# Attention probabilities turned in one step, one batch's queries loaded in 128-byte blocks, and a new count of warm matmuls in the opening

## The chip, the cores and the metric

The kernel runs on one core of a Trainium2 chip. TensorE (PE) multiplies matrices into PSUM, VectorE (DVE) and ScalarE (ACT) do what is done element by element, GpSimd (POOL) a few subtractions, and SyncE (SP) issues the DMAs. The metric is the device time of one execution in microseconds (us), as the median of several runs.

## The reference

Two attentions in a row, then a mixture of experts with one expert per token. B=8, H=8, S=576, D=64, 32 packs; the experts take 512 features through F=1024, E=8.

```
p_packed = softmax(scale * p @ k.T) @ v          # 32 packs attend to 576 keys
x        = softmax(scale * q @ p_packed.T) @ p_packed
for each token s of batch b:
    fresh  = argmax(x[b, s] @ w_gate)
    e      = fresh if s == 0 or sigmoid(x[b, s] @ w_local) < 0.5 else expert of token s-1
    prob   = softmax(x[b, s] @ w_gate)[e]
    out[b, s] = prob * (relu(x[b, s] @ w1[e]) @ w2[e])
```

## The kernel before

All eight batches go through one pipeline. For each batch, whose tokens take one expert in the usual case, the kernel does not form x. It packs the expert's W1 with the attended packs (`pack_weights`: ppT times a 512-wide half of W1, a "pack", L783; ACT rounds it to wph at L790, DVE keeps the rest as wpl at L793), so that layer 1 multiplies the query probabilities a2 straight into the packed weights. Both sides are kept as a high and a low part (a2h, a2l; wph, wpl), so one half of a 128-wide chunk of layer 1 is six matmuls (L806, "a six"). Its relu gives h (high part on ACT L816, low part on DVE L821). W2 is split likewise (ACT L832, DVE L834), and layer 2 sums h times W2 into five accumulators acc0 to acc4 (L845, L850, L854). A batch has eight chunks, each with two sixes and five blocks of layer 2.

Beside these main matmuls PE does the next batches' attention, as side work:

- `scores` (L415): packs times keys, into two banks.
- `keys`: exp of the scores (ACT L448), then the probabilities are turned, 2 times 3 transposes of 128 by 96 (L458), each three into one PSUM bank, copied by ACT (L460) to a1T; times the values (L470, "av"); divided on DVE into zz (L478); turned on PE (L485) and copied to ppT.
- `queries`: query scores (L511, L520), DVE transposes to sT (L529), maximum (L540), subtraction (L542), exp on ACT (L544), sum (L548, L550, L552), division (L554), transposes into a2t (L560), then a2h (ACT L568) and a2l (L571; on DVE for batch 0, on POOL for the others).
- Queries and keys come to PE with their features on the partitions. For batches 0 and 1 they are loaded as tokens, rows of 1536 bytes (`load_tokens`, L274), and turned by PE three transposes at a time (`turn_tokens`, L365) with an ACT copy (L369); for later batches they are loaded as blocks in runs of 128 bytes (`load_blocks`, four DMAs at L288) and turned by DVE (`turn_keys`, `turn_queries`).

PSUM has three working banks, bank0 to bank2, and the five accumulators; before batch 0's main matmuls begin, the accumulators serve as further banks. A bank is free again when what reads it is done. The order on each engine is fixed when the kernel is built: `weave` runs all of these as generators, each of which says with `need` what it waits for (tiles, buffers, so many banks), and a planner (`Clock`) that prices each instruction gives the time at which each could go on. The main thread `chunks` is taken when it is ready, the side threads when their time has come and a credit allows. Anything that alters one planned time can alter the order from there on. Before batch 0's main matmuls begin, `weave` also fills PE's planned pauses with `keep_warm(n)`: n matmuls of a zero tile (L214), whose results are not used.

`FIRST_W2` holds back loads: in batch 0 the pieces of W2 from number 2 on wait for batch 1's values, those from number 4 on for its queries; in batch 1 the values and queries wait for as many pieces of W2.

Of the kernel before, what the change touches and what calls it, by code (L numbers as in the profile page):

```python
# [38 lines left out]
WARM, FILL = 10, 400.0  # L39
# [119 lines left out]
def packed_attn_moe_kernel(  # L159
# [156 lines left out]
    def loads(st):  # L316
# [11 lines left out]
        else:  # L328
            if isinstance(b, int):
                yield need(when=lambda: "loaded" in sts[b - 1] and (b < 2 or "ereg" in sts[b - 2]))  # L330
            order = (("p", 1), ("k", 0), ("k", 1), ("v", 0), ("v", 1), ("q", 0), ("q", 1)) if st["second"] else \
                (("v", 0), ("v", 1), ("p", 1), ("k", 1), ("q", 1))
        for name, Q in order:
            blocks = name in "kq" and not (st["early"] or st["second"])
            if st["second"] and name in FIRST_W2:
                yield need(when=lambda: len(sts[0].get("w2", ())) >= FIRST_W2[name])
            yield need(slot="p_in" if name == "p" else "qn" if blocks else "kv")
            if name == "p":
                st["p"] = load_packs_by_half(b)
                continue  # L340
            x = {"k": k, "v": v, "q": q}[name]
            if blocks:
                st[name] = load_blocks(x, b)
            else:
                st[name, Q] = load_tokens(x, b, Q)
# [96 lines left out]
    def keys(st, Q):  # L442
# [11 lines left out]
        for r in range(2):  # L454
            yield need(sc, banks=1, when=lambda: not st["early"] or st["weighed"] == NQ)
            tp = bank()
            for j in range(J3):
                nc.tensor.transpose(out=tp[:TP, 128 * j:128 * j + 128], in_=chunks[:, (J3 * r + j) // 2, (J3 * r + j) % 2], identity=ident)  # L458
            copy = nc.vector.tensor_copy if st["early"] and r == 1 else nc.scalar.copy
            copy(out=a1T[:, J3 * r:J3 * r + J3], in_=tp[:TP, :128 * J3].rearrange("a (j x) -> a j x", j=J3))  # L460
            give(tp)
        give(sc)
# [36 lines left out]
    def queries(st, Q):  # L499
# [56 lines left out]
        for r in range(2):  # L556
            if st["early"] or st["second"]:
# [190 lines left out]
    def weights(st):  # L748
# [10 lines left out]
        for c in range(NC):  # L759
            if st.get("early"):  # L760

                yield need(when=lambda: all(c < n or (x, 1) in sts[1] for x, n in FIRST_W2.items()))
# [186 lines left out]
    def weave(main):  # L949
# [3 lines left out]
        while main in threads or any(x.batch < 0 for x in threads):  # L953
# [4 lines left out]
            while started < B and started <= max(at_batch[0], 0) + AHEAD:  # L958
# [3 lines left out]
                    *((turn_keys(st, 0), turn_keys(st, 1)) if started != 1 else (turn_keys(st, 0), turn_tokens(st, "k"))), scores(st, 0), scores(st, 1), keys(st, 0), keys(st, 1), gate_weights(st) if started == 0 else None, gates(st), *((turn_queries(st, 0), turn_queries(st, 1)) if started > 1 else (turn_tokens(st, "q"),)), queries(st, 0), queries(st, 1),  # L962
# [17 lines left out]
            if x is None:  # L980
                x = min(when, key=when.get)
                if at_batch[0] < 0:
                    keep_warm(max(0, int((when[x] - now) / FILL)))
# [113 lines left out]
```

## Time and profile before

| | before |
|---|---|
| median of 3 runs | 440.71 us (440.34 to 441.14) |
| the profiled execution | 440.03 us, its span 438.2 us |
| PE busy | 417.8 us, 95% |
| DVE busy | 303.9 us, 69% |
| ACT busy | 183.5 us, 42% |
| mean granted clock of PE | 0.984 |
| chain that ended last | PE 88%, DVE 5%, DMA 3% |

The span is cut at PE's work by the profile: a row of the views below gives an instruction (or a run of alike ones), its start in us from the span's start, its duration, its line in the code, and in brackets how long the engine stood idle just before it and what ended that. Busy times of PE in a row overlap with those of its neighbours, since matmuls are pipelined; what a group takes is read from start to start. The granted clock is 1.00 at 2.4 GHz and 0.50 at 1.2 GHz. A matmul in float32 has several records: a warm matmul has two.

### The profile page before, as it was taken

The page shows a single profiled execution, that of the slowest core. Times are in us where ns is not written, and L with a number is a line of the kernel's source. Part 1 is how long each engine was busy: PE and PEld are TensorE (multiplying, and loading weights), DVE is VectorE, ACT ScalarE, POOL GpSimd, SP SyncE. Part 2 cuts the span into 40 slices and gives each one's busy share as a digit, 9 for nine tenths or more (in the row PEclk, how much of TensorE's full clock was granted, in tenths as well). Part 3 has the DMA queues.
Part 4 walks back from the last instruction along what each step waited for, and adds up shares of the span by engine and source line. Part 5 has one row for each costly group of instructions (what it writes and reads, how often), then busy time and mean ns, then how long its engine had stood idle before and what let it go on. Part 6 is the DMA issues. An engine that isn't in the chain of part 4 may idle for free.

```text
span 438.2 us, 10127 instructions
## 1 busy us (share of the span) xinstructions
PE 417.8 (95%) x3928; PEld 326.9 (75%) x3929; DVE 303.9 (69%) x831; ACT 183.5 (42%) x424; POOL 24.9 (6%) x41
## 2 busy tenths in 40 slices
PE   7968999999999999999999999999999999999993
PEld 6756778758866787588876787587876788688882
DVE  4587469876986798648984898648985798444331
ACT  1544534454435553535425553435424453443231
POOL 0000002100110011000110011000110002000000
PEclk9896999999999999999999999999999999999998
DMA  8989699899939995999269991999455210921003
GB/s 191 233 266 259 174 148 137 327 182 226 96 121 321 133 142 179 349 131 194 94 220 240 177 194 49 347 140 141 157 187 186 81 43 10 351 96 37 0 1 114
DMA packets 153942, 73.16 MB, mean 167 GB/s; under 512 B 123680, under 2 KB 132896, under 8 KB 153888
## 3 DMA queue, kind: packets, MB, share of 16 engines
q1 hardware_dynamic: 151760, 72.30, 75.5%
q8 instruction: 33, 0.54, 0.6%
q10 hardware_dynamic: 2128, 0.15, 0.4%
q14 instruction: 21, 0.17, 0.2%
HBM read 63.00 MB, written 9.44 MB: 165 GB/s over the span
## 4 chain that ended last, share of the span: by engine, by line
PE 88%; DVE 5%; DMA 3%; issue 1%; ACT 1%; SPq 0%; POOLq 0%; DVEq 0%; POOL 0%; ACTq 0%
PE acc L845 40%; PE bank L806 24%; PE acc L850 4%; PE bank L783 3%; DMA kv<-in_k_dram 3%; PE acc L854 3%; PE bank L470 3%; PE bank L415 2%; PE bank L458 2%; PE bank L511 2%; PE bank L658 1%; DVE wpl L793 1%; PE bank L365 1%; DVE a2t L560 1%; PE acc L214 0%
## 5 line engine op out<-in xcount | busy, mean ns | idle before, releaser
L845 PE MATMUL acc<-w2s,h 128*128 128x512 f32 x768 | 207.7, 402 | 0.0
L845 PEld LDWEIGHTS acc<-w2s,h 128*128 128x128 f32 x768 | 135.1, 188 | 30.6 <-issue 8.3
L816 ACT ACTIVATE h<-bank 128x288 fp32r<-128x288 f32 x128 | 52.7, 412 | 117.9 <-PE bank L806 108.1
L821 DVE SCALAR_TENSOR_TENSOR h<-bank,h 128x288 fp32r<-128x288 f32 (+2 forms) x192 | 61.3, 347 | 50.1 <-ACT h L816 49.3
L806 PEld LDWEIGHTS bank<-a2h,wph 128*128 128x128 f32 x256 | 47.0, 191 | 23.9 <-issue 3.6
L806 PE MATMUL bank<-a2h,wph 128*128 128x288 f32 x256 | 57.9, 308 | 5.5 <-DVE wpl L793 1.8
L806 PE MATMUL bank<-a2l,wph 128*128 128x288 f32 x256 | 55.5, 299 | 0.0
L806 PE MATMUL bank<-a2h,wpl 128*128 128x288 f32 x256 | 55.3, 298 | 0.0
L834 DVE TENSOR_TENSOR w2s<-w2raw,w2s 128x512 fp32r<-128x512 f32 x64 | 47.7, 745 | 8.3 <-ACT w2s L832 8.2
L806 PEld LDWEIGHTS bank<-a2l,wph 128*128 128x128 f32 x256 | 41.7, 191 | 0.0
L806 PEld LDWEIGHTS bank<-a2h,wpl 128*128 128x128 f32 x256 | 41.7, 191 | 0.0
L832 ACT CAST w2s<-w2raw 128x512 fp32r<-128x512 f32 x64 | 39.4, 616 | 0.2
L571 POOL TENSOR_TENSOR a2l<-a2t,a2h 128x576 fp32r<-128x576 f32 x14 | 20.5, 1462 | 328.7 <-ACT a2h L568 328.7
L793 DVE TENSOR_TENSOR wpl<-bank,wph 128x512 fp32r<-128x512 f32 x31 | 20.1, 685 | 13.3 <-ACT wph L790 13.3
L790 ACT CAST wph<-bank 128x512 fp32r<-128x512 f32 x31 | 16.7, 590 | 28.0 <-PE bank L783 26.9
L850 PE MATMUL acc<-w2s,h 128*128 128x512 f32 x64 | 26.9, 420 | 0.0
L854 PE MATMUL acc<-w2s,h 128*64 128x512 f32 x64 | 25.3, 395 | 0.0
L783 PE MATMUL bank<-w1t,ppT 64*32 64x512 f32 x248 | 17.4, 601 | 2.7 <-DVE sm L550 1.6
L529 DVE STREAM_TRANSPOSE sT<-bank 128x288 f32<-128x288 f32 x30 | 12.8, 462 | 10.1 <-ACT gate L527 9.4
L448 ACT ACTIVATE a<-a,nb 128x576 f32<-128x576 f32 x16 | 12.5, 779 | 14.9 <-DVE nb L433 14.9
L460 ACT COPY a1T<-bank 96x384 f32<-96x384 f32 x28 | 13.3, 477 | 10.5 <-PE bank L458 10.0
L383 DVE STREAM_TRANSPOSE qn<-qn 128x1152 f32<-128x1152 f32 x12 | 16.4, 1364 | 0.1
(146 smaller groups left out, 434.7 us busy)
## 6 DMA issues: line engine op xcount, KB each, us to landing
w1t<-in_moe_w_dram SPq DMA_DIRECT2D x16, 1024.0 KB, 6.3
w2raw<-in_moe_w_dram SPq DMA_DIRECT2D x64, 256.0 KB, 7.7
kv<-in_v_dram SPq DMA_DIRECT2D x16, 576.0 KB, 10.7
out_dram<-o SPq DMA_DIRECT2D x32, 256.0 KB, 3.8
qn<-in_k_dram SPq DMA_DIRECT2D x24, 288.0 KB, 7.5
qn<-in_q_dram SPq DMA_DIRECT2D x24, 288.0 KB, 6.9
kv<-in_k_dram SPq DMA_DIRECT2D x4, 576.0 KB, 6.9
kv<-in_q_dram SPq DMA_DIRECT2D x4, 576.0 KB, 11.2
```

Source lines behind the costliest of these rows:

```text
L571: eng.tensor_tensor(out=a2l, in0=a2t, in1=a2h.bitcast(F32), op=ALU.subtract)
L783: nc.tensor.matmul(out=ts[Q][32 * h:32 * h + 32, :], lhsT=st["ppT"][Q][rows, 32 * h:32 * h + 32], rhs=w1t[rows, h], start=True, stop=True,)
L790: nc.scalar.copy(out=hi[:, Q], in_=ts[Q])
L793: nc.vector.tensor_tensor(out=lo[:, Q], in0=ts[Q], in1=hi[:, Q].bitcast(F32), op=ALU.subtract)
L806: nc.tensor.matmul(out=t[:, :HALF], lhsT=st["wp"][c // 4][wi][:, Q, fs], rhs=a2[ai][Q][:, ts], start=(n == 0), stop=(n == 5),)
L816: nc.scalar.activation(out=h[:, HALF * half:HALF * half + HALF], in_=t[:, :HALF], func=AF.Relu)
L821: nc.vector.scalar_tensor_tensor(out=h[:, dst:dst + z - a], in0=t[:, a:z], scalar=0.0, in1=h[:, HALF * half + a:HALF * half + z].bitcast(F32),
L832: nc.scalar.copy(out=w[:, 0], in_=raw)
L834: nc.vector.tensor_tensor(out=w[:, 1], in0=raw, in1=w[:, 0].bitcast(F32), op=ALU.subtract)
L845: nc.tensor.matmul(out=acc, lhsT=hs[hi], rhs=w[:, wi], start=(c == 0 and n == 0), stop=(c == NC - 1 and n == 2),)
L850: nc.tensor.matmul(out=acc, lhsT=h[:, 512:S + TAIL], rhs=w[:, 0], start=(c == 0), stop=False, skip_group_check=True,)
L854: nc.tensor.matmul(out=acc[0:TAIL], lhsT=h[:, 512:S], rhs=w[:, 1], start=False, stop=(c == NC - 1), skip_group_check=True,)
```

## The change

1. `keys` turns both halves of the probabilities in one step: it asks for two banks at once, issues the six transposes in a row into both, and then the two copies. Before, each half asked for one bank, was turned and copied, and only then the other.
2. Batch 1's queries are loaded as blocks and turned by DVE (`turn_queries`), as in later batches, in place of tokens turned by PE. Two "kv" buffers are no longer used for them, one "qn" buffer is. The layout of a2t for batch 1 follows. The condition that holds back W2's pieces of batch 0 names the new load. Batch 1's keys stay tokens.
3. Before batch 0's main matmuls, the number of warm matmuls is the time from PE's planned end (no longer from `now`) to the next planned step, divided by 240 in place of 400.

```diff
-WARM, FILL = 10, 400.0
+WARM, FILL = 10, 240.0
...
-            order = (("p", 1), ("k", 0), ("k", 1), ("v", 0), ("v", 1), ("q", 0), ("q", 1)) if st["second"] else \
+            order = (("p", 1), ("k", 0), ("k", 1), ("v", 0), ("v", 1), ("q", 1)) if st["second"] else \
                 (("v", 0), ("v", 1), ("p", 1), ("k", 1), ("q", 1))
         for name, Q in order:
-            blocks = name in "kq" and not (st["early"] or st["second"])
+            blocks = name in "kq" and not st["early"] and not (st["second"] and name == "k")
...
-        for r in range(2):
-            yield need(sc, banks=1, when=lambda: not st["early"] or st["weighed"] == NQ)
+        def turned(r):
             tp = bank()
             for j in range(J3):
                 nc.tensor.transpose(out=tp[:TP, 128 * j:128 * j + 128], in_=chunks[:, (J3 * r + j) // 2, (J3 * r + j) % 2], identity=ident)
+            return tp
+
+        def copied(r, tp):
             copy = nc.vector.tensor_copy if st["early"] and r == 1 else nc.scalar.copy
             copy(out=a1T[:, J3 * r:J3 * r + J3], in_=tp[:TP, :128 * J3].rearrange("a (j x) -> a j x", j=J3))
             give(tp)
+
+
+        yield need(sc, banks=2, when=lambda: not st["early"] or st["weighed"] == NQ)
+        for r, tp in enumerate([turned(r) for r in range(2)]):
+            copied(r, tp)
         give(sc)
...
-            if st["early"] or st["second"]:
+            if st["early"]:
...
-                yield need(when=lambda: all(c < n or (x, 1) in sts[1] for x, n in FIRST_W2.items()))
+                yield need(when=lambda: all(c < n or x in sts[1] for x, n in ((("v", 1), FIRST_W2["v"]), ("q", FIRST_W2["q"]))))
...
-                    ... ((turn_queries(st, 0), turn_queries(st, 1)) if started > 1 else (turn_tokens(st, "q"),)), ...
+                    ... ((turn_queries(st, 0), turn_queries(st, 1)) if started else (turn_tokens(st, "q"),)), ...
...
-                    keep_warm(max(0, int((when[x] - now) / FILL)))
+                    keep_warm(max(0, int((when[x] - clock.engine("PE")) / FILL)))
```

In the new kernel the lines behind `keys` are numbered seven higher (L783 becomes L790, L806 L813, L845 L852, and so on; the turn L458 is L457). The planner puts the work in another order nearly everywhere. Three places follow, by the fixed order of the two kernels; a row is a line, an operation, what it writes, what it reads, its shape, and how many stand in a row.

On PE, batch 0's two packs and the first six of layer 1, before (L783 the pack, the two halves of W1 being w1t_451 and w1t_453; L214 warm matmuls):

```order
L365 MATMUL bank2_513<-ident_77,kv_315 128x96 x3
L214 MATMUL acc4_66<-warm_64 128x128
L783 MATMUL bank0_535<-w1t_451,ppT_313 32x512 x4
L783 MATMUL acc1_536<-w1t_451,ppT_324 32x512 x4
L214 MATMUL acc4_66<-warm_64 128x128 x5
L783 MATMUL bank1_565<-w1t_453,ppT_313 32x512 x4
L783 MATMUL bank2_566<-w1t_453,ppT_324 32x512 x4
L806 MATMUL bank0_583<-a2h_123,wph_533 128x288
```

and now:

```order
L365 MATMUL acc1_561<-ident_77,kv_333 128x96 x3
L790 MATMUL bank0_567<-w1t_470,ppT_331 32x512 x4
L790 MATMUL bank1_568<-w1t_470,ppT_342 32x512 x4
L214 MATMUL acc4_66<-warm_64 128x128 x10
L790 MATMUL bank2_620<-w1t_472,ppT_331 32x512 x4
L790 MATMUL bank0_621<-w1t_472,ppT_342 32x512 x4
L813 MATMUL bank1_632<-a2h_123,wph_565 128x288
```

Ten warm matmuls stand between the packs where five did, and the last quarter goes to bank0, which the first quarter of the first pack wrote; before, no bank came twice.

On DVE, what follows batch 0's a2t at the same place, before (wpl the packs' low parts, w2s the low part of W2's first piece, h the first relu):

```order
L560 STREAM_TRANSPOSE a2t_122<-sT_406 128x3x96 x2
L571 TENSOR_TENSOR a2l_125<-a2t_121,a2h_123 128x576
L571 TENSOR_TENSOR a2l_126<-a2t_122,a2h_124 128x576
L793 TENSOR_TENSOR wpl_534<-bank0_535,wph_533 128x512
L793 TENSOR_TENSOR wpl_534<-acc1_536,wph_533 128x512
L793 TENSOR_TENSOR wpl_564<-bank1_565,wph_563 128x512
L793 TENSOR_TENSOR wpl_564<-bank2_566,wph_563 128x512
L834 TENSOR_TENSOR w2s_590<-w2raw_455,w2s_590 128x512
L821 SCALAR_TENSOR_TENSOR h_562<-bank0_583,h_562 128x288
```

and now:

```order
L567 STREAM_TRANSPOSE a2t_122<-sT_436 128x3x96 x2
L578 TENSOR_TENSOR a2l_125<-a2t_121,a2h_123 128x576
L578 TENSOR_TENSOR a2l_126<-a2t_122,a2h_124 128x576
L800 TENSOR_TENSOR wpl_566<-bank0_567,wph_565 128x512
L800 TENSOR_TENSOR wpl_566<-bank1_568,wph_565 128x512
L841 TENSOR_TENSOR w2s_639<-w2raw_474,w2s_639 128x512
L800 TENSOR_TENSOR wpl_615<-bank2_620,wph_614 128x512
L800 TENSOR_TENSOR wpl_615<-bank0_621,wph_614 128x512
L828 SCALAR_TENSOR_TENSOR h_613<-bank1_632,h_613 128x288
```

W2's low part moved from behind the last two wpl to ahead of them. Further up on DVE, the maximum of the first quarter's scores moved ahead of the transposes of the second quarter's.

On PE, batch 1's attention beside batch 0's second chunk of layer 2 (L458 a turn, L365 queries' tokens, L470 av, L485 the turn of zz), before:

```order
L458 MATMUL bank2_778<-ident_77,a1_579 96x128 x3
L365 MATMUL bank1_788<-ident_77,kv_478 128x96 x3
L845 MATMUL acc0_643<-w2s_630,h_601 128x512 x3
L470 MATMUL bank2_795<-kv_461,a1T_758 32x64 x24
L365 MATMUL bank1_824<-ident_77,kv_478 128x96 x3
L845 MATMUL acc1_662<-w2s_630,h_601 128x512 x3
L485 MATMUL bank2_848<-ident_77,zz_820 128x128
L365 MATMUL bank0_853<-ident_77,kv_518 128x96 x3
L845 MATMUL acc2_680<-w2s_630,h_601 128x512 x3
```

and now:

```order
L492 MATMUL bank2_812<-ident_77,zz_800 128x128
L852 MATMUL acc0_693<-w2s_681,h_653 128x512 x3
L457 MATMUL bank1_821<-ident_77,a1_618 96x128 x3
L457 MATMUL bank2_825<-ident_77,a1_618 96x128 x3
L852 MATMUL acc1_712<-w2s_681,h_653 128x512 x3
L852 MATMUL acc2_730<-w2s_681,h_653 128x512 x3
L477 MATMUL bank0_843<-kv_480,a1T_816 32x64 x24
```

The token transposes are gone, the two threes of the turn stand together, and two blocks of layer 2 lie between them and the av that reads their copies. In all, the order of before has 11 of 18 turns with their halves side by side, that of now all 18; warm matmuls ahead of the first scores go from 19 to 30. At the seam between batches 0 and 1 the new order has both packs of batch 1 in batch 0's last half chunk, the first on bank0 and bank1, the second on bank2 and bank0; in batches 3 to 6 the order is now the same from batch to batch. On SP, the values of batch 2 follow W2's pieces directly.

## Rows read from the trace of the kernel before

**Rows 1.** The page, part 1: engine, busy us, share of the span, instructions.
```profile
PE 417.8 (95%) x3928; PEld 326.9 (75%) x3929; DVE 303.9 (69%) x831; ACT 183.5 (42%) x424; POOL 24.9 (6%) x41
```

**Rows 2.** By stretch: length, each engine's busy us, PEclk, DMA share, GB/s.
```profile
11.50:14.80 3.30, 3.30 (x27) 2.87 (x14) 1.29 (x8) 2.21 (x5) 0.00 (x0) 0.50 1.10 235
28.60:35.30 6.70, 3.50 (x42) 1.62 (x42) 6.55 (x14) 4.59 (x11) 0.00 (x0) 1.00 1.06 350
35.40:42.10 6.70, 5.95 (x50) 5.57 (x51) 4.80 (x11) 2.17 (x5) 0.00 (x0) 0.50 1.08 262
50.00:60.00 10.00, 8.76 (x122) 7.10 (x121) 3.74 (x10) 4.57 (x14) 0.00 (x0) 1.00 0.79 151
135.00:430.00 295.00, 293.80 (x2545) 230.86 (x2544) 206.53 (x540) 127.17 (x288) 16.14 (x20) 1.00 0.69 152
```

**Rows 3.** PE's waits: line, releaser, us in total, times, longest us.
```profile
PE bank L806 <- DVE zz L478: 1.4, 3, 0.5
...
PE bank L806 <- DVE df L716: 0.8, 1, 0.8
PE bank L806 <- ACT qn L369: 0.7, 1, 0.7
...
PE bank L806 <- ACT a1T L460: 0.5, 1, 0.5
```

**Rows 4.** PE in time, opening: start, us, engine, line, tiles, count [idle <- releaser].
```profile
1.09 6.18 PE L214 MATMUL acc<-warm 128*128 128x128 f32 x38 [1.09 <-DVE warm L207]
8.80 1.15 PE L415 MATMUL acc<-kv,p_in 32*32 32x192 f32 x48 [1.53 <-DVE p_in L351]
...
23.57 0.44 PE L365 MATMUL acc<-ident,kv 96*128 96x96 f32 x3 [1.28 <-DMA kv<-in_k_dram]
```

**Rows 5.** PE in time, first packs and first layers.
```profile
33.54 1.09 PE L783 MATMUL bank<-w1t,ppT 64*32 64x512 f32 x16 [1.10 <-DMA w1t<-in_moe_w_dram]
36.15 0.82 PE L806 MATMUL bank<-a2h,wph 128*128 128x288 f32 x2 [1.52 <-DVE wpl L793]
...
42.13 0.89 PE L845 MATMUL acc<-w2s,h 128*128 128x512 f32 x3
```

**Rows 6.** DVE in time, batch 0's queries and packs.
```profile
24.75 0.48 DVE L529 STREAM_TRANSPOSE sT<-acc 128x288 f32<-128x288 f32 x1 [0.96 <-PE bank L511]
...
25.52 1.37 DVE L540 TENSOR_REDUCE mx<-sT 128x18 f32<-128x576 f32 x2
...
34.64 0.76 DVE L571 TENSOR_TENSOR a2l<-a2t,a2h 128x576 fp32r<-128x576 f32 x1 [0.15 <-ACT a2h L568]
...
36.52 1.28 DVE L793 TENSOR_TENSOR wpl<-bank,wph 128x512 fp32r<-128x512 f32 x2
...
38.41 0.46 DVE L821 SCALAR_TENSOR_TENSOR h<-bank,h 128x288 fp32r<-128x288 f32 x1
```

**Rows 7.** ACT in time, casts of the second packs and of W2.
```profile
34.66 1.07 ACT L790 CAST wph<-bank 128x512 fp32r<-128x512 f32 x2
35.62 0.63 ACT L832 CAST w2s<-w2raw 128x512 fp32r<-128x512 f32 x1
```

**Rows 8.** PE in time, one of batch 1's eight token transposes.
```profile
52.36 0.41 PE L365 MATMUL bank<-ident,kv 96*128 96x96 f32 x3
52.56 0.94 PE L845 MATMUL acc<-w2s,h 128*128 128x512 f32 x3
```

**Rows 9.** By stretch, columns as in rows 2: token loads, then block loads.
```profile
40.20:45.60 5.40, 5.40 (x66) 3.55 (x59) 3.28 (x11) 1.17 (x3) 0.00 (x0) 0.82 1.09 233
58.50:72.50 14.00, 14.00 (x101) 11.88 (x100) 12.44 (x29) 6.19 (x15) 1.51 (x1) 1.00 1.42 138
```

**Rows 10.** PE in time, a turn of six in a later batch.
```profile
232.26 0.42 PE L806 MATMUL bank<-a2h,wph 128*128 128x288 f32 x2
...
233.06 0.82 PE L458 MATMUL bank<-ident,a 128*96 128x128 f32 x6
233.63 0.94 PE L845 MATMUL acc<-w2s,h 128*128 128x512 f32 x3
```

More of the change, by code (lines that the diff above doesn't have):

```diff
@@ L961, in weave @@
                     slots(st), pack_weights(st), *((early_choice(st),) if started == 0 else ()),
-                    *((turn_keys(st, 0), turn_keys(st, 1)) if started != 1 else (turn_keys(st, 0), turn_tokens(st, "k"))), scores(st, 0), scores(st, 1), keys(st, 0), keys(st, 1), gate_weights(st) if started == 0 else None, gates(st), *((turn_queries(st, 0), turn_queries(st, 1)) if started > 1 else (turn_tokens(st, "q"),)), queries(st, 0), queries(st, 1),
+                    *((turn_keys(st, 0), turn_keys(st, 1)) if started != 1 else (turn_keys(st, 0), turn_tokens(st, "k"))), scores(st, 0), scores(st, 1), keys(st, 0), keys(st, 1), gate_weights(st) if started == 0 else None, gates(st), *((turn_queries(st, 0), turn_queries(st, 1)) if started else (turn_tokens(st, "q"),)), queries(st, 0), queries(st, 1),
                 ) if g is not None)
```

## Prediction

> **What bounds the kernel now.** I read the busy times first: TensorE (PE) works 417.8 us of a span of 438.2 [rows 1], so the kernel can gain only where PE stands idle, runs at a lower clock, or does work that can be dropped. The table by stretch says where that is: from 135 us on PE is busy 293.80 of 295.00 us, at full clock, while between 28.6 and 35.3 us it is busy 3.50 of 6.70, and from 35.4 to 42.1 it is busy but at a granted clock of 0.50, which is the lower of its two levels, 1.2 GHz [rows 2]. The list of PE's waits then names what ends each pause; those that the change can touch after 50 us are the two on ScalarE copies (0.7 and 0.5 us) and four on small VectorE steps (zz 1.4 in three waits, df 0.8) [rows 3]. Last come the stretches themselves, in order of time [rows 4 to 8].
>
> **The sum's base.** The profiled execution took 440.03 us, the median of the three runs is 440.71, 0.68 more. All terms below are differences against the profiled execution; I add them to the median.
>
> **Opening, to 24 us.** Eleven more warm matmuls (30 in place of 19) stand ahead of the first scores. The nineteen took 6.18 us (38 records, two to a matmul), so eleven take at most 3.6, which from 7.27 us is 10.9, against 8.80 where the scores began behind a pause of 1.53 us [rows 4]. The scores come up to 2.0 us late, less if the clock was up by then. Against that, the clock stood at 0.50 from 11.5 to 14.8 [rows 2], behind that pause; with the pause closed it should stay up, which gives back up to half of those 3.3 us. And what follows is set by transfers: at 23.57 PE still waited 1.28 us for the second batch's keys [rows 4], which no edit moves. Term: 0, between -0.3 (a little of the gain passes that wait) and +0.4 (some of the delay does).
>
> **First packs, 24 to 42 us.** VectorE's chain here is the softmax of batch 0's queries; it idles 0.96 us before the second pair of transposes and then does two maxima in 1.37 us [rows 6]. The new order does the first maximum in that pause: the chain ends 0.64 us earlier, so the last a2l (34.64 plus 0.76) ends at 34.76 in place of 35.40 [rows 6]. But the second half's pack now takes bank0 for its second quarter, the bank of the first half's first quarter, since the spare accumulators are no longer picked. It must wait for the first wpl, which two steps of 0.64 us apart [rows 6] puts at 35.4. From there everything is serial. The pair of packs took 1.09 us [rows 5], and one alone cannot be much cheaper as the two ran side by side: to 36.45. ScalarE's cast (two in 1.07) and the split of W2 (0.63) [rows 7] end at 37.6; VectorE now does W2's low part, the same operation on as many elements as a wpl, ahead of the last two wpl (0.64 each) [rows 6]: 38.3, 38.95, 39.6; a relu low part (0.46 [rows 6]) follows, to 40.1. PE: the first layer-1 six at 36.45, 0.80 us at full clock [rows 10], to 37.25; the second waits for the third wpl, 39.0 to 39.8; the gate matmuls wait for the fourth, and are done at about 40.45; the third six to 41.25. Layer 2 starts near 41.5, where it started at 42.13 [rows 5]. That holds if the clock stays up, for which I see two reasons: ten warm matmuls fill 31 to 33.6 where five did, and the pack and its layer 1 follow. Term: -0.6; it is +1.3 if the clock falls in the new pause (a rival).
>
> **Batch 1's queries, 42 to 62 us.** Gone are eight groups of three transposes on PE. Busy times of these overlap with neighbours, so I count from start to start: 52.36 to 52.56 is 0.20 us [rows 8]; the eight, all between 48 and 60.3, come to 1.88. Gone too is the wait for the copy of one of them (0.73), and that for a1T (0.5), since the two halves of a turn now follow each other and their copies finish behind layer 2 rather than ahead of layer 1 [rows 3]. In their place VectorE turns the blocks in two transposes, each of four times as many elements as the one at 24.75 (0.48 [rows 6]), so at most 1.9 us, in a stretch where it is busy 3.74 of 10 us [rows 2]: hidden, and if that cover were gone it would be up to 3.8 us on the chain of the query scores. Term: -3.1, between -3.6 and -1.9 (only the transposes go).
>
> The blocks come in runs of 128 bytes. Token rows moved at 233 GB/s between 40.2 and 45.6 us, blocks of the third batch at 138 between 58.5 and 72.5 [rows 9]: 1.18 MB take 8.5 us in place of 5.1. Issued at the same place in SyncE's queue, behind W1 and four pieces of W2, they land 3.4 us after the token stretch ended, at 49.0. The turns stand in VectorE's order behind the first zz, near 50 us by the walk above (an estimate). Cost 0 while that holds. "The Trainium skill, DMA: Bandwidth & Descriptors, Specifications" asks for transfers of at least 512 bytes and says that smaller ones turn into a read-modify-write; the 138 against 233 GB/s agrees in direction. By that rule alone the edit would be a loss on the transfer, and it becomes one on the clock only if something waits for it: a rival below.
>
> SyncE also loses a wait: batch 2's values were loaded only when batch 1's values had been used; with two buffers spared they go at once. Nothing on PE waited for them. Cost 0.
>
> **Turn in one step, everywhere.** Six transposes together take 0.57 us (233.06 to 233.63), and layer 2 follows with no pause [rows 10]: the joined form already occurs. By the order, 11 of 18 pairs stood together before and all 18 do now. It costs PE nothing. What it can cost is layer 1 a bank: two of three are held until their copies are done. Where the order puts layer 2 behind a turn, that is hidden.
>
> **Seam from batch 0 to 1, near 84 us.** The second half's pack again takes bank0 right behind the first half's, with fourteen small VectorE steps in the order ahead of the wpl that frees it. If that wpl comes late, the two quarters no longer run side by side: one alone takes about as long as the two together, 1.0 us more on PE [rows 5], and a wait of some 0.2 us, an estimate, comes on top. Term: +1.2, between 0 (VectorE is ahead) and +1.7 (a wait of 0.7).
>
> **Batches 2 to 7.** The planner lays them out anew; three zz waits and one df wait [rows 3] need not recur. Half of the 2.2 us: -0.8 after a few more changes between large and small tiles; between -2.2 and +0.6.
>
> **Sum.** 0 - 0.6 - 3.1 + 1.2 - 0.8 = -3.3 us: 440.7 - 3.3 = **437.4 us**.
>
> **Rivals.**
> *The clock falls in the new pause* at 37.3 to 39.0. For: it did in the same place, after pauses of 1.10 and 1.52 us [rows 5]. Against: PE is much busier between 31 and 37 now. Layer 2 then starts at 43.4, as 36.15 to 42.13 was run at the lower level [rows 2, 5]: 1.9 us worse than the forecast, 439.3.
> *All later pauses go*: the planner, which now prices turns as single steps, leaves no zz or df wait, and the seam costs nothing. 437.4 - 1.4 - 1.2 = 434.8. For: from 135 us on there is only 1.2 us of idle time left [rows 2]. Against: three banks for as much work as before.
> *Blocks slow what lies ahead of them.* The second half's pack already waited 1.10 us for W1 [rows 5], and the blocks are under way beside W1's tail and W2. If their 3.4 us land on W1 or on the first W2, layer 2 starts that much later: 440.8, no change. For: the stretch is at a DMA share above 1 [rows 2]. Against: W1 is issued first.
> *Slower: joined turns starve layer 1.* Each of 14 turns of batches 1 to 7 holds two of three banks until ScalarE has copied both, and layer 1 needs one for each half chunk; where it finds none it waits about as long as for zz, 0.47 us. 14 times 0.47 is 6.6: 444.0. It decides from 0.24 us per turn on. For: the zz waits are of this kind. Against: the row at 233.06, where layer 2 covers the copies [rows 10].
> *The change doesn't do what it says*: the order shows the transposes gone and the pairs joined, so it gets no chance of its own.
>
> **Chances.** Forecast 0.46; clock falls 0.20; all pauses go 0.10; blocks slow 0.12; starving 0.12. A measurement of this kernel tells about 0.2% from no change, 439.8 to 441.6. The clock case lies at that bound, three quarters of it faster: faster 0.46 + 0.15 + 0.10 = 0.71; same 0.05 + 0.12 = 0.17; slower 0.12. The range leaves out starving and the lower half of the case without pauses: 434.4 to 441.3, which also holds the forecast with its terms at their ends, short of all at once.
>
> **What would show it.** The profile of the changed kernel should have PE's first layer 2 near 41.5 us with a pause of 1.5 to 2 us before it on a wpl, full clock from 15 us on, no copies of tokens after 35 us, 61 us' place in the order reached some 3.6 us earlier, a pause before the seam's pack on a wpl, and batches 3 to 6 as before to 0.5 us each. I am wrong if the clock is at 0.50 anywhere behind 15 us, if PE waits for W1 or W2 of batch 0 by more than 2 us, or if layer 1 waits on a1T or zz in most batches.

## The result, and the profile after

| | before | changed | 
|---|---|---|
| median | 440.52 us (440.04 to 441.14, 4 runs) | 434.18 us (433.41 to 434.98, 4 runs) |
| ratio | | 0.9866, 95% interval 0.9844 to 0.9888 |
| profiled execution | 440.03 us, span 438.2 | 433.41 us, span 431.7 |

The change takes 6.3 us off by the medians (434.18 is 0.9856 of 440.52), 5.9 by the ratio on record, which is not the quotient of these two medians. The forecast was 437.4, 3.3 us less than before: the right side, a little over half the size. The lower end that was given, 434.4, lies between the two readings: the median is 0.2 us below it, 0.9866 of the forecast's base of 440.71 is 434.8. So the result stands at the edge of the range.

Three views answer to those shown of before. PE's busy time on the page [rows 1] rises by 2.8 us, to 97% of a shorter span (the added warm matmuls are in it):

```profile
PE 420.6 (97%) x3976; PEld 330.2 (76%) x3977; DVE 303.6 (70%) x833; ACT 180.8 (42%) x416; POOL 24.3 (6%) x41
```

By stretch, columns as in [rows 2]: the clock is now at its higher level between 11.5 and 14.8 us, and between 28.6 and 35.3 PE is busy nearly throughout; from 35.4 to 42.1 it idles 1.57 us, and the clock is at its lower level for a part of the stretch; from 135 us on 0.09 us of idle time is left, against 1.20:

```profile
11.50:14.80 3.30, 3.30 (x69) 2.79 (x68) 1.59 (x10) 1.74 (x4) 0.00 (x0) 1.00 1.09 252
28.60:35.30 6.70, 6.42 (x65) 4.44 (x63) 6.48 (x14) 3.92 (x9) 0.00 (x0) 1.00 1.06 342
35.40:42.10 6.70, 5.13 (x53) 3.65 (x53) 2.80 (x5) 2.61 (x6) 0.00 (x0) 0.77 1.22 218
135.00:424.00 289.00, 288.91 (x2531) 228.39 (x2516) 202.74 (x536) 123.57 (x279) 16.11 (x20) 1.00 0.69 151
```

In the list of PE's waits, the four that stood in [rows 3] are gone (zz, df and the two on copies), though 0.64 us on another small VectorE step (gsm) now stands where the 0.81 on df stood, behind the same score (at 126.05 us, 128.96 before); a wpl holds PE twice, where the forecast said that it would:

```profile
PE bank L813 <- DVE wpl L800: 1.6, 1, 1.6
...
PE bank L813 <- DVE gsm L732: 0.6, 1, 0.6
PE bank L790 <- DVE wpl L800: 0.4, 1, 0.4
PE acc L365 <- DMA kv<-in_k_dram: 0.3, 1, 0.3
```

Where the time went is read best by landmarks. I take the start of ACT's relu of one half chunk of layer 1, the same one in both kernels, and subtract. In the profiled execution the changed kernel stands 0.92 us *behind* the kernel before at batch 0's second chunk, 2.66 us ahead at its fifth (67.47 us before), 2.76 at its seventh, 2.59 at batch 1's fifth, 3.50 at batch 2's fifth, 4.71 at batch 4's, 5.88 at batch 6's and 5.94 at the end of batch 7. So the opening lost 0.9 us, the stretch of batch 1's queries gave 3.6, the seam cost nothing net, and batches 1 to 6 gave another 3.3. The last 0.6 us of the difference of the spans lie behind the last layer 2 and are not explained by the change: from the last relu of batch 7 to the end of the span the kernel before took 13.95 us, the changed one 13.34, and the other profiles of this study, whatever their edits, 13.25 to 13.81.

### The profile page after: what moved, and what is told of

Its sections match the earlier page's. It is cut to its first block, busy times and chain, and to the rows that moved or that the text cites. A ratio compares the mean times of both kernels' runs of the same rounds, so it can differ in the third digit from the quotient of the medians.

```text
span 431.7 us, 10241 instructions
## 1 busy us (share of the span) xinstructions
PE 420.6 (97%) x3976; PEld 330.2 (76%) x3977; DVE 303.6 (70%) x833; ACT 180.8 (42%) x416; POOL 24.3 (6%) x41
## 4 chain that ended last, share of the span: by engine, by line
PE 94%; DVE 2%; DMA 1%; ACT 1%; issue 0%; POOLq 0%; POOL 0%; DVEq 0%; ACTq 0%
PE acc L852 42%; PE bank L813 25%; PE bank L790 4%; PE acc L857 4%; PE acc L214 4%; PE acc L861 3%; PE bank L477 3%; PE bank L457 2%; PE bank L415 2%; PE bank L518 2%; DMA kv<-in_k_dram 1%; PE bank L665 1%; ACT wph L797 0%; PE bank L492 0%; PE acc L365 0%; DVE a2l L578 0%
## 5 line engine op out<-in xcount | busy, mean ns | idle before, releaser
L852 PE MATMUL acc<-w2s,h 128*128 128x512 f32 x768 | 207.1, 401 | 0.0
L852 PEld LDWEIGHTS acc<-w2s,h 128*128 128x128 f32 x768 | 135.0, 188 | 26.8 <-issue 4.1
L813 PEld LDWEIGHTS bank<-a2h,wph 128*128 128x128 f32 x256 | 46.2, 190 | 25.0 <-issue 5.8
L813 PE MATMUL bank<-a2h,wph 128*128 128x288 f32 x256 | 58.2, 309 | 2.6 <-DVE wpl L800 1.6
L813 PE MATMUL bank<-a2l,wph 128*128 128x288 f32 x256 | 55.0, 296 | 0.0
L813 PE MATMUL bank<-a2h,wpl 128*128 128x288 f32 x256 | 54.8, 296 | 0.0
L841 DVE TENSOR_TENSOR w2s<-w2raw,w2s 128x512 fp32r<-128x512 f32 x64 | 44.4, 694 | 3.2 <-ACT w2s L839 3.1
L813 PEld LDWEIGHTS bank<-a2l,wph 128*128 128x128 f32 x256 | 41.2, 189 | 0.0
L813 PEld LDWEIGHTS bank<-a2h,wpl 128*128 128x128 f32 x256 | 41.2, 189 | 0.0
L214 PE MATMUL acc<-warm 128*128 128x128 f32 x146 | 21.1, 297 | 1.1 <-DVE warm L207 1.1
L214 PEld LDWEIGHTS acc<-warm 128*128 128x128 f32 x146 | 19.2, 208 | 2.3 <-issue 1.4
L790 PE MATMUL bank<-w1t,ppT 64*32 64x512 f32 x256 | 19.3, 601 | 0.4 <-DVE wpl L800 0.4
L503 DVE STREAM_TRANSPOSE qn<-qn 128x1152 f32<-128x1152 f32 x14 | 19.2, 1371 | 0.0
```

The costliest lines, as they stand in the source:

```text
L214: nc.tensor.matmul(out=warm_ps[:, :128], lhsT=warm, rhs=warm, start=True, stop=True)
L790: nc.tensor.matmul(out=ts[Q][32 * h:32 * h + 32, :], lhsT=st["ppT"][Q][rows, 32 * h:32 * h + 32], rhs=w1t[rows, h], start=True, stop=True,)
L813: nc.tensor.matmul(out=t[:, :HALF], lhsT=st["wp"][c // 4][wi][:, Q, fs], rhs=a2[ai][Q][:, ts], start=(n == 0), stop=(n == 5),)
L841: nc.vector.tensor_tensor(out=w[:, 1], in0=raw, in1=w[:, 0].bitcast(F32), op=ALU.subtract)
L852: nc.tensor.matmul(out=acc, lhsT=hs[hi], rhs=w[:, wi], start=(c == 0 and n == 0), stop=(c == NC - 1 and n == 2),)
```

## The experiments

All runs of the kernel before beside these experiments have medians of 440.3 to 440.4 us, in a spread of 438.3 to 443.9. Single executions of one kernel differ by a microsecond or two, in some kernels by five to seven, and the profiles show where: ahead of batch 0's fifth chunk, in the stretch that waits for the first loads. From that landmark on, two executions of one kernel agree within 0.03 us, in each of the three kernels that were profiled twice. So beside the medians I give two numbers for each kernel, from its profiled execution against that of before: the lead at batch 0's fifth chunk (negative is ahead), and what was added to it from there to the end.

| kernel | median us | lead at batch 0's fifth chunk | added from there to the end |
|---|---|---|---|
| changed; again | 434.18; 434.21 | -2.66; -1.23 | -3.28; -3.25 |
| warm count alone | 439.19 | -0.21 | -0.80 |
| joined turn alone | 436.13 | +0.20 | -3.79 |
| blocks alone; again | 435.96; 436.38 | +2.15; -1.74 | -0.96; -0.94 |
| changed, old warm count | 434.41 | -1.77 | -2.03 |
| changed, split turn | 436.82 | -1.00 | -0.92 |
| changed, tokens | 438.30 | -0.72 | -2.45 |
| changed, warm matmuls in the pause | 434.12 | -3.15 | -3.27 |
| changed, second pack in accumulators; again | 432.64; 433.02 | -5.13; -3.52 | -3.25; -3.26 |
| the same, planner told a lower rate | 435.57 | -5.58 | +4.81 |

**One part alone.** Three kernels put one part of the change into the kernel before. The warm count:

```diff
-WARM, FILL = 10, 400.0
+WARM, FILL = 10, 240.0
...
-                    keep_warm(max(0, int((when[x] - now) / FILL)))
+                    keep_warm(max(0, int((when[x] - clock.engine("PE")) / FILL)))
```

> The kernel before with the new count of warm matmuls alone. Theory, the parts add up: the packs come to stand on bank0 twice as in the changed kernel (layer 2 starts near 43 us, not 42.1), the token transposes stay, the later batches gain little: 440.5 to 442 us. Rival, the later gain of the changed kernel (3.3 us behind the seam) comes from a new order of any kind: 437 to 438.5 us.

Measured: 439.19 us (ratio 0.9988, interval 0.9960 to 1.0017, not told from no change). Neither theory: less than the kernel before by 1.1 us, of which the landmarks give 0.8 to the later batches.

The turn in one step:

```diff
-        for r in range(2):
-            yield need(sc, banks=1, when=lambda: not st["early"] or st["weighed"] == NQ)
...
+        yield need(sc, banks=2, when=lambda: not st["early"] or st["weighed"] == NQ)
+        for r, tp in enumerate([turned(r) for r in range(2)]):
+            copied(r, tp)
```

> The kernel before with the turn in one step alone. Theory: this part carries the gain of the later batches (pauses on zz and on score banks go): 3 to 3.5 us less, and half a microsecond in batch 1 (the wait on a1T), 436.7 to 437.7 us; PE's pauses on zz are gone from its list of waits. Rival, the gain is that of any new order: 439 to 441 us, zz waits still there.

Measured: 436.13 us, ratio 0.9886 (0.9858 to 0.9914). The theory's mechanism holds, with half a microsecond more than its range, and the rival falls: the lead grows by 3.79 us behind batch 0's fifth chunk, and zz and df are gone from PE's list, columns as in [rows 3]. What is left at the top of it comes from the opening:

```profile
PE bank L813 <- DVE wpl L800: 1.6, 1, 1.6
```

The blocks, with the layout, W2's condition and the thread list that go with them:

```diff
-            blocks = name in "kq" and not (st["early"] or st["second"])
+            blocks = name in "kq" and not st["early"] and not (st["second"] and name == "k")
...
-                    ... if started > 1 else (turn_tokens(st, "q"),)), ...
+                    ... if started else (turn_tokens(st, "q"),)), ...
```

> The kernel before with batch 1's queries as 128-byte blocks alone. Theory: 1.9 us of transposes and 0.7 us of a wait on a copy go, nothing waits for the blocks: 437.5 to 438.5 us. Rival, the blocks slow W1 or W2 of batch 0: 439 to 441 us, and PE waits for a w1t or a w2s in the opening. Second rival, a new order of any kind gives 3 us more: 435 us.

Measured: 435.96 us, ratio 0.9899 (0.9838 to 0.9960). The size fits neither: more than the theory's 2.6 us, less than the second rival's 5. The profiled execution was by far the longest of its five (440.75 us), and PE's two longest waits in it are these:

```profile
PE bank L485 <- DVE zz L478: 2.6, 1, 2.6
PE bank L783 <- DMA w1t<-in_moe_w_dram: 2.6, 1, 2.6
```

The second is the first rival's mark, but in an execution that stands for itself. The first contradicts the theory that nothing waits for the blocks: VectorE stood 3.84 us for their landing, at the turn that its order has ahead of that zz, and from 57.1 to 63.9 us PE's clock was at its lower level. VectorE in time, then PE's stretch, columns as in [rows 2]:

```profile
56.53 1.38 DVE L496 STREAM_TRANSPOSE qn<-qn 128x1152 f32<-128x1152 f32 x1 [3.84 <-DMA qn<-in_q_dram]
```

```profile
57.00:64.00 7.00, 5.81 (x38) 4.09 (x39) 4.26 (x8) 1.51 (x5) 0.00 (x0) 0.51 1.13 223
```

The same kernel was run once more for a profile of an ordinary execution:

> The kernel before with the blocks alone, once more, for a profile of an ordinary execution. Theory, the wait of 2.6 us for W1 in its first profile came with a lower clock and a late load in that one execution: a wait for W1 of 1 to 1.5 us as in the kernel before, 436 us, 3 us ahead of the kernel before at the fifth chunk of batch 0. Rival, the blocks do slow W1: a wait of 2.5 us again.

Measured: 436.38 us (435.82 to 437.48). There is no wait for W1 at all; PE's longest wait is for the first piece of W2's split on ACT:

```profile
PE bank L806 <- ACT w2s L832: 1.7, 1, 1.7
```

So the blocks do not slow W1 as a rule. VectorE waited 0.50 us for them here, and PE not at all: from the second chunk of batch 0 to the fifth this execution gained 3.63 us on the kernel before, where the first one lost 1.77. The lead of 1.74 us at the fifth chunk is less than the 3 that the expectation named, since this execution was 1.89 us behind at the second chunk, after an opening at a lower clock (below).

**One part undone.** The same three edits, taken back one at a time from the changed kernel (each diff above, read from + to -).

> The changed kernel with the old count of warm matmuls. Theory, the new count is worth nothing net (it closes small pauses up to 24 us, and its order of packs costs 2 us of pauses and clock by 43 us): 433.5 us within 1, layer 2 starting near 42 us, no wait of a pack for a wpl. Rival, it is worth its own 1.1 us again: 435.3 us. Second rival, without the pack's wait the gains add: 432 us.

Measured: 434.41 us, ratio 0.9850 (0.9812 to 0.9887): no net worth of the new count can be told. But it does what it is meant to do, as the table by stretch shows, columns as in [rows 2]. First the changed kernel with the old count, then the second profile of the blocks alone, which has the old count too:

```profile
14.90:28.50 13.60, 11.90 (x198) 7.61 (x198) 5.74 (x23) 4.38 (x14) 0.00 (x0) 0.64 0.80 161
```

```profile
14.90:28.50 13.60, 11.78 (x198) 7.54 (x197) 5.62 (x22) 4.49 (x14) 0.00 (x0) 0.65 0.78 163
```

All three kernels of this study with the old count (four profiles) have a clock of 0.64 to 0.75 between 14.9 and 28.5 us; the profile of the kernel before, with 1.00 there, is the exception (its low stretch came earlier, 11.5 to 14.8 us [rows 2]). All nine profiles with the new count have 1.00 there.

Where that gain is lost again is not shown. As expected, no pack waits for a wpl with the old count; but layer 2 started at 43.89 us, not near 42, in the slowest of the four executions. Behind batch 0's fifth chunk the old count adds 1.25 us less, and its list of PE's waits names a reason that the changed kernel does not have, two waits of the seam's packs for batch 1's W1:

```profile
PE bank L790 <- DMA w1t<-in_moe_w_dram: 1.4, 2, 1.0
```

> The changed kernel with the turn in two steps. Theory, the gain behind the seam is what the joined turn brings and other new orders bring only a part of: at the seam 2.7 us ahead of the kernel before as with all three, at the end 3.5 to 4.5 us: 436 to 437 us, with waits on zz back. Rival, the parts add without it (warm 1.1 and blocks 4.4): 434.8 us. Second rival, any new order brings it: 434.2 us.

Measured: 436.82 us, ratio 0.9900 (0.9866 to 0.9934), inside the theory's range. The lead behind the fifth chunk is 0.92 us in place of 3.28, and waits on zz are back:

```profile
PE bank L806 <- DVE zz L478: 0.9, 2, 0.5
```

At the seam it was 0.9 us ahead of the kernel before, not the 2.7 that the expectation reckoned with; its clock was at the lower level from 38.9 to 45.7 us.

> The changed kernel with batch 1's queries as tokens. Theory: nothing of the 3 us between 42 and 62 us is left, the later gain is: 436.8 us within 0.8, with the wait on a token copy (0.7) back. Rival, the parts add (warm 1.1, joined 4.2): 435 us.

Measured: 438.30 us (436.46 to 441.22), ratio 0.9962 (0.9935 to 0.9990). More than the theory's upper end of 437.6. Its order is another again, and adds 2.45 us behind the fifth chunk, not 3.28; the wait on a token copy that was expected is not in its list.

**The bank taken twice, and the clock behind it.** Layer 2 started at 43.08 us where the forecast said 41.5. Two kernels bear on the pause and on the clock. The first fills the pause and leaves the order as it is:

```diff
                     yield need(hi, lo, *st["a2h"], *st["a2l"], banks=1)
+                    if isinstance(b, int) and b == 0 and c == 0 and half == 1:
+                        nc.pop_inst_callback()
+                        keep_warm(7)
+                        nc.push_inst_callback(clock.note)
```

> The changed kernel with seven warm matmuls in the pause of 1.56 us between the first two sixes of layer 1, the order otherwise the same. Theory, the clock falls because of this pause: it stays at 1.00 from 36 to 42 us, the two sixes and the gate matmuls run at full speed, 1.5 us less than the changed kernel, about 432.7 us. Rival, the clock falls for what was before it (the wait of 0.38 and the small tiles): no change, 434.2 us. Second rival, what PE gains it waits for DVE or ACT again: 433.7 us or more.

PE in time, and its stretch from 35.4 to 42.1 us:

```profile
38.27 1.72 PE L214 MATMUL acc<-warm 128*128 128x128 f32 x14
39.99 0.53 PE L813 MATMUL bank<-a2h,wph 128*128 128x288 f32 x2
...
42.59 0.86 PE L852 MATMUL acc<-w2s,h 128*128 128x512 f32 x3
```

```profile
35.40:42.10 6.70, 6.32 (x77) 4.49 (x70) 4.04 (x8) 2.92 (x6) 0.00 (x0) 1.00 1.17 235
```

The mechanism is as expected: the clock stays at 1.00, and from the second six to layer 2 it takes 2.60 us (39.99 to 42.59) in place of 4.06 (39.02 to 43.08 in the changed kernel), 1.46 less. The time does not show it: 434.12 us (432.99 to 437.33), as the changed kernel; single executions differ by more. That the clock falls *because* of the pause is not settled either. Five profiles have this pause unfilled (1.55 to 1.56 us): in three the clock fell (the changed kernel twice, the split turn), in two it did not (the warm count alone, the tokens), so one profile with the pause filled and the clock up proves little. The changed kernel with tokens:

```profile
36.27 1.06 PE L790 MATMUL bank<-w1t,ppT 64*32 64x512 f32 x8 [0.38 <-DVE wpl L800]
...
39.89 0.54 PE L813 MATMUL bank<-a2h,wph 128*128 128x288 f32 x2 [1.55 <-DVE wpl L800]
...
42.49 0.86 PE L852 MATMUL acc<-w2s,h 128*128 128x512 f32 x3
```

The second gives the pack other banks, so that none is taken twice; the planner then also lays out another order around it:

```diff
-            ts = [bank() for Q in range(NQ)]
+            ts = [psum(x) for x in ("acc3", "acc2")] if st["early"] and fh == 1 else [bank() for Q in range(NQ)]
```

> The changed kernel with the second pack of batch 0 in two accumulators, so that no bank is taken twice. Theory, the pauses of 0.38 and 1.56 us and the lower clock behind them come from the bank taken twice: layer 2 starts near 40 us in place of 43.1, and 3 us less at the end: 431.2 us. Rival, the next thing is late instead (W2's first piece on DVE, the values of batch 1): half of it, 432.7 us. Second rival: the new order costs it again behind the seam, 434 us.

Measured: 432.64 us (431.14 to 437.98). PE in time: the pack's quarters run side by side again, scores stand behind them and the gate matmuls ahead of the second six (at 37.50), and layer 2 starts at 39.90, 3.2 us earlier. The place is the theory's, the time the first rival's:

```profile
34.40 1.09 PE L790 MATMUL acc<-w1t,ppT 64*32 64x512 f32 x16
35.28 1.25 PE L415 MATMUL bank<-qn,p_in 64*32 64x288 f32 x16
...
39.90 1.55 PE L852 MATMUL acc<-w2s,h 128*128 128x512 f32 x6
```

The same kernel again, and the changed kernel beside it on the same chip:

> The changed kernel once more, beside the next two on the same chip: 434.2 us within 0.7.

> The changed kernel with the second pack of batch 0 in two accumulators, once more beside the changed kernel: theory, 2.0 to 2.5 us less than it, about 432 us; rival, its one slow run was typical and the mean gain is under 1 us.

Measured: 434.21 us (432.41 to 434.88) and 433.02 us (430.94 to 436.83). Layer 2 started at 44.52 and 40.42 us. The lead at the fifth chunk is 2.5 and 2.3 us larger than the changed kernel's, first with first and second with second; but the two profiles of either kernel differ by 1.4 and 1.6 in it, so the size of the gain is open. The medians differ by 1.2 to 1.5 us, the means of these last two runs by 0.2 (433.9 and 433.7), as the rival had it, and three of ten executions are slower than any of the changed kernel's nine. So it is the fastest version by its median, and not shown to be faster. Nor is the bank told from the rest of the new order. In the second profile a six of layer 1 stands still in its middle, for nothing that the profile names:

```profile
46.02 0.29 PE L813 MATMUL bank<-a2h,wph 128*128 128x288 f32 x1 [1.73 <-issue]
```

The list of PE's waits in the first one has a new leader, 1.4 us on a zz. VectorE stood before that zz, at the turn of the blocks, and those had not landed (in the second profile it stood 2.33 us for them):

```profile
51.75 1.38 DVE L503 STREAM_TRANSPOSE qn<-qn 128x1152 f32<-128x1152 f32 x1 [3.13 <-DMA qn<-in_q_dram]
53.05 0.31 DVE L485 TENSOR_SCALAR zz<-bank,rs 128x128 f32<-128x128 f32 x1
```

**The blocks' landing.** The last kernel tells the planner that they take longer, so that it puts their turn behind that zz:

```diff
-        clock.rate = 150.0
+        clock.rate = 90.0 if isinstance(b, int) and b == 1 else 150.0
```

> As the one before, and the planner is told a lower rate for batch 1's blocks (90 in place of 150), so that their turn stands behind the second zz and one chunk later on VectorE. Theory, the wait of 1.36 us on that zz was VectorE waiting for the blocks' landing: it goes, 1.0 to 1.5 us less than with the accumulators alone, 430.8 us. Rival, what is put off comes late at the seam: no gain, 432 us.

Measured: 435.57 us (433.41 to 439.06), 2.6 us slower than with the accumulators alone. The theory's wait is gone, and the lead at the fifth chunk is the largest of all (-5.58), but its time did not come. The rival's mechanism did, and cost more than it gave: in this profile, the slowest of the six, the lead is lost at the seam, where batch 1's packs, scores and turns now come too late, and where the clock then was at its lower level for 10.2 of 13.7 us (columns as in [rows 2]):

```profile
PE bank L790 <- ACT ppT L495: 1.1, 1, 1.1
...
PE bank L457 <- ACT a L448: 0.9, 1, 0.9
PE bank L415 <- DVE h L828: 0.8, 1, 0.8
```

```profile
86.30:100.00 13.70, 12.60 (x103) 7.55 (x104) 9.75 (x35) 5.97 (x14) 0.00 (x0) 0.63 1.12 307
```

## Why the forecast was right in direction and too small

The mechanisms were the forecast's own, and the sizes were not. By the landmarks of the profiled execution the terms came out so, with the forecast in brackets: to the start of layer 2, +0.9 us (-0.6); batch 1's queries, -3.6 (-3.1); the seam, 0 (+1.2); what follows, -3.3 (-0.8); behind the last relu, -0.6 (not forecast). The mis-sized term above all is that of the later batches, by 2.5 us; that the time came out no farther off is partly luck, since the first packs erred by 1.5 us the other way than all the rest.

**Opening to 24 us** (0): as forecast. The scores began at 9.78 us in place of 8.80, and the wait for batch 1's keys, which a transfer ends, shrank from 1.28 us [rows 4] to 0.3.

**First packs** (-0.6): the walk was right, and the choice of clock wrong. The pack's last quarter started at 35.41 (forecast 35.4), the first six at 36.40 (36.45), the second at 39.02 (39.0), held by the third wpl, with W2's low part ahead of it on VectorE:

```profile
33.96 1.06 PE L790 MATMUL bank<-w1t,ppT 64*32 64x512 f32 x8
35.41 1.06 PE L790 MATMUL bank<-w1t,ppT 64*32 64x512 f32 x8 [0.38 <-DVE wpl L800]
36.40 0.53 PE L813 MATMUL bank<-a2h,wph 128*128 128x288 f32 x2
...
39.02 0.85 PE L813 MATMUL bank<-a2h,wph 128*128 128x288 f32 x2 [1.56 <-DVE wpl L800]
...
40.76 1.08 PE L665 MATMUL bank<-a2t,gate 128*32 128x128 f32 x16
...
43.08 0.86 PE L852 MATMUL acc<-w2s,h 128*128 128x512 f32 x3
```

```profile
34.66 1.28 DVE L800 TENSOR_TENSOR wpl<-bank,wph 128x512 fp32r<-128x512 f32 x2
37.67 0.69 DVE L841 TENSOR_TENSOR w2s<-w2raw,w2s 128x512 fp32r<-128x512 f32 x1 [1.72 <-ACT w2s L839]
38.28 1.28 DVE L800 TENSOR_TENSOR wpl<-bank,wph 128x512 fp32r<-128x512 f32 x2
```

But the six at 39.02 takes 1.74 us to the gate matmuls at 40.76, at half clock, where 0.80 was reckoned. Layer 2 came at 43.08, 0.95 us later than before, near the 43.4 of the rival in which the clock falls. The step that failed here is the sentence that gave two reasons for the clock to stay up: the ten warm matmuls did fill 31.5 to 33.9, and it fell all the same, at 39.0 us, for 3.4 us. That was one of the forecast's own signs of being wrong (0.50 anywhere behind 15 us).

**Batch 1's queries** (-3.1): the lead moves by 3.58 us between the second and the fifth chunk. From start to start, summed by line over the stretches that answer to each other (42.1 to 425.5 us before, 43.05 to 419.6 after), the token transposes are 1.87 us before and gone now, the query gate matmuls, with the pause on a token copy behind them, take 0.81 us less, and the first two turns of zz, with the pause on a1T behind one of them, 0.84 less. These are the three things that the forecast named, and nearly all of the gain. With tokens put back, the lead at the fifth chunk is between 0.5 and 1.9 us smaller. What the forecast had wrong here is the landing, 49.0 us. The last of the blocks' four loads landed at 51.87 in the changed kernel. Most of the difference is the base: the forecast took the end of the token stretch, 45.6, but the second token load of the kernel before landed at 47.79, so that the blocks were 4.1 us behind the tokens, and the price by bytes, 3.4, was not far off. The rest shows in SP's queue and in the DMA share. The four issues of the blocks took 16.47 us from first to last, the tokens' two 3.66, and in both the second issue began just as W1's second half had landed (33.5 and 33.3 us). First before, then now:

```profile
30.15 3.66 SPq L274 DMA_DIRECT2D kv<-in_q_dram  x2
```

```profile
29.99 16.47 SPq L288 DMA_DIRECT2D qn<-in_q_dram  x4
```

The blocks' second issue alone lasted 9.61 us, to 42.92. From 42.0 on what had been issued was through, and the DMA engines stood nearly idle for 1.5 us (the last three numbers are PE's clock, the DMA share and GB/s):

```profile
39.00:42.00 3.00, 2.98 (x39) 2.58 (x39) 0.93 (x2) 0.92 (x2) 0.00 (x0) 0.50 1.43 163
42.00:43.50 1.50, 1.50 (x13) 1.46 (x9) 1.35 (x4) 0.22 (x1) 0.00 (x0) 0.86 0.14 13
43.50:50.10 6.60, 6.60 (x97) 4.22 (x100) 3.44 (x15) 2.94 (x9) 0.00 (x0) 1.00 1.42 145
```

In the changed kernel the turn stood at 52.56, 0.7 us behind the landing, so nothing waited; with the accumulators, 2.5 us further ahead, something did. "The Trainium skill, DMA: Bandwidth & Descriptors, Specifications" was the warning here (runs under 512 bytes): the trace agrees that such a load is slow (145 GB/s in the longest of the three stretches, against 233 for the tokens [rows 9]), and that this costs time only where something waits.

**Seam** (+1.2): the mechanism happened, the loss is elsewhere made up. The second pack's quarters ran one after the other, 1.92 us in place of 1.09 (0.83 more), with no pause on top:

```profile
85.38 1.09 PE L790 MATMUL bank<-w1t,ppT 64*32 64x512 f32 x16
...
87.05 1.92 PE L790 MATMUL bank<-w1t,ppT 64*32 64x512 f32 x16
88.90 0.53 PE L813 MATMUL bank<-a2h,wph 128*128 128x288 f32 x2
```

The lead stays within 0.2 us across the seam all the same, mostly because the pause of 0.47 us on a zz that stood behind it is gone.

**Batches 2 to 7** (-0.8): this is the term that was mis-sized most. The lead grows by 3.28 us behind batch 0's fifth chunk. Summed by line from there to the end: the av matmuls with the pauses behind them 1.47 us less, the scores 1.37, the turns of zz 1.09, layer 2 some 0.6; against these the seam's pack 0.83 more and the layer 1 matmuls 0.40 more. The first is the pauses on zz, of which the forecast gave half; they all went. The second was not in the forecast at all. A score's two halves go to two banks; here they run side by side in most scores and one after the other in some, and the list of waits does not show that, since PE works. One score before, with the VectorE steps that read a bank just then, and the same score now:

```profile
273.44 1.47 PE L415 MATMUL bank<-qn,p_in 64*32 64x288 f32 x16
274.84 0.97 PE L845 MATMUL acc<-w2s,h 128*128 128x512 f32 x3
```

```profile
273.64 0.48 DVE L821 SCALAR_TENSOR_TENSOR h<-bank,h 128x224 fp32r<-128x224 f32 x2
```

```profile
269.67 0.72 PE L415 MATMUL bank<-qn,p_in 64*32 64x288 f32 x16
270.32 0.96 PE L852 MATMUL acc<-w2s,h 128*128 128x512 f32 x3
```

It is 1.40 us from start to start in place of 0.65. Before, its first eight matmuls start from 273.44 to 273.73 and the other eight only from 274.22 on, 0.1 us behind the end of the relu at 274.12; now all sixteen start within 0.35 us. That the relu held the second half's bank is read from these times; no run tests it. Two of twelve scores were so before (1.40 and 1.02), none is now; the rest of the 1.37 is the pause behind another score that shrank from 0.81 (df) to 0.64 (gsm). Every profile with the split turn has both, the one of 1.40 and the one of 1.02 (the changed kernel with the turn split again is shown); of those with the joined turn up to the last kernel none has the one of 1.40, and with the joined turn alone the one of 1.02 is there:

```profile
271.59 1.47 PE L415 MATMUL bank<-qn,p_in 64*32 64x288 f32 x16
```

Which part does it is shown: the three kernels with the split turn add 0.80 to 0.96 us, those with the joined turn 2.03 to 3.79 (the last kernel aside; the 2.03 has the 1.4 us of waits for W1 in it). So the joined turn is worth 2.4 us there in the changed kernel, and some 0.9 us come with each of the new orders that keep the split turn. The forecast had batches 3 to 6 as before to 0.5 us each; from one fifth chunk to the next the lead grew by 0.66, 0.55, 0.84 and 0.33.

**Rivals.** The starving of layer 1 by turns that hold two banks did not happen: no wait of layer 1 on a1T is in the list. The blocks did not slow W1 in the ordinary execution; their own landing can cost PE time, as the first profile of the blocks alone showed. The clock case was right in its place, and was paid for by the later batches. The case in which all later pauses go was priced at 434.8 and given one chance in ten; it came nearest to the time, and its mark, no wait on zz or df, is in the list above. But its pauses are not all of the gain: the zz waits were 1.4 us, df gave way to gsm, the seam's pack cost 0.83 and not nothing, and the slow scores were not in it.

**The parts do not add.** Alone they take 1.1, 4.4 (or 3.9) and 4.2 us off the kernel before, 9.2 to 9.7 together, and the change 6.3. The later batches show why: 0.80, 0.95 and 3.79 us there sum to 5.5, and together they give 3.3. In part they remove the same pauses: the zz waits of layer 1 were 1.4 us before [rows 3], 0.9 with the warm count alone or the blocks alone, and none with the joined turn alone.

## What to carry to other kernels

A list of waits under-counts what a better order can give: matmul groups that run side by side in one order and one after the other in another lose time without PE being idle, so sum each line from start to start, too. Where a planner lays out the work, a change in one place is a new order everywhere, and single parts neither add nor can be read off one another; landmarks (the same instruction in both traces) tell a lasting gain from a shift in the opening that differs between executions. A load of many short pieces is to be priced from the landing of what it replaces, not from the end of a busy stretch, and with its issue time; its slack is gone as soon as something else ahead of it gets faster.

## What the runs showed of the hardware

Issuing a 1.18 MB load in four pieces of 128-byte runs took SP's queue 15.4 to 16.7 us from first to last in the opening (ten profiles), the same bytes in two pieces of 1536-byte rows 3.0 to 3.7 (four profiles); some 2 to 3 us of either lie between the first issue and the second. PE's clock in the opening is not the same in every execution of one kernel: with the blocks alone it was 1.00 between 28.6 and 35.3 us in one profile and 0.69 in the other. The nine profiles with more warm matmuls show 1.00 between 14.9 and 28.5 us, four of the five with fewer 0.64 to 0.75. A pause of 1.55 to 1.56 us on PE was followed by half clock in three profiles and by full clock in two. Scores whose two halves ran one after the other took 1.40 us from start to start in place of 0.65, with no idle time of PE.
